# Float64 weights to float32 in three word operations instead of four, the first of them a Prelu on ScalarE

## The chip, the cores and the metric

One core of a Trainium2 chip runs the whole program. The core has a matrix engine (TensorE, PE in the rows; its weight loads are PEld), VectorE (DVE), ScalarE (ACT), GpSimd (POOL) and SyncE (SP), which issues all the DMAs here. The metric is the time of one execution on the device, in microseconds (us).

## The reference

Attention with a decay, then two feed-forward blocks that run over all tokens:

```python
scores = scale * q @ k.T;  decay = cumsum(log(clip(f)))        # 4 batches x 8 heads, 576 x 576, head size 64
x = softmax(causal(scores + decay)) @ v                        # -> 2304 tokens x 512
h = x @ moe_w_in;   x = (h * clip(h + 3, 0, 6) / 6) @ moe_w_out          # 512 -> 2048 -> 512
h = x @ moe2_w_in;  out = softplus(h) @ moe2_w_out                       # 512 -> 2048 -> 512
```

`moe_w_in`, `moe_w_out` and `moe2_w_in` come as float64 after their scaling, and the kernel makes float32 of float64 words itself. All the rest is float32.

## The kernel before

**Stages.** Attention goes through 4 batches of 4 head pairs. The first block runs over token tiles of 512 (the last one 256), with 16 tiles of 128 hidden features each; its first tokens need only batch 0 of the attention, so the matmuls of the block (lines 1299 and 1362) are mixed with the attention's (685, 776, 846) up to some 490 us. The second block, with sums and differences of its tiles prepared in advance (lines 1415 and 1516), fills the span from some 640 us to the end.

**Order.** Every operation is put into a list with its operands, a wish time `at` and one or more ways (an engine with an assumed cost). `Work.order` then sends them one by one to the engine that could start first by these costs, and so writes one fixed order for each engine. On the chip each engine goes through its own list strictly in order, and a semaphore holds it where an operand is not ready. Nothing else sets the times, so an instruction that waits holds up all that stands behind it on its engine.

**Weights.** There are 64 tiles of 128 x 512 float64 words to convert, two 32-bit words each. A tile is loaded by one 512 KB DMA into a staging buffer, `st0` or `st1` for 62 tiles and two places of `HY` for 2; eight of the tiles, of the second block, are converted late, from 570 us on. `raw_weights` converts it in four operations, whose names in the code are:

- `conv0` (line 1016 or 1017): the upper word, read as a float32, times 2^-112, which brings its exponent field to float32's. The planner may choose DVE or ACT; in the order before, 63 of 64 are on ACT.
- `conv1` (line 1019, DVE): the lower word shifted right by 29.
- `conv2` (line 1020, DVE): the upper word shifted left by 3, or'ed with that.
- `conv3` (line 1023, DVE): the sign bit of the upper word, or'ed in.

For the first block `weights` then rounds the tile to the matmul's type on ACT (line 1035) and subtracts that from the tile on POOL (line 1036); only then can the next load into the same staging buffer land. `early2` converts 24 tiles of the second block during the first and stores them to DRAM.

**Around it.** DVE also holds the running minimum of the scores (line 701), the low halves of the transposed probabilities (816), of Q and K (632) and of the hidden activations (1322), the product behind the activation (1341), and copies that the planner may give to ACT or DVE: the rounded hidden tile (1319 on ACT, 1320 on DVE) and copies of the halves of Q and K (643 on ACT, 645 on DVE).

Of the kernel before, what the change touches and what calls it, by code (L numbers as in the profile page):

```python
# [10 lines left out]
U32 = mybir.dt.uint32  # L11
ACTF = mybir.ActivationFunctionType
ALU = mybir.AluOpType
# [36 lines left out]
    pc=794.25,  # L50
# [21 lines left out]
    cvw=29.86,  # L72
# [33 lines left out]
class Work:  # L106
# [11 lines left out]
    def op(self, ways, fn=None, r=(), w=(), after=(), at=0.0, banks=(), hold=(), free=(), nbytes=0, name="", seq=None, from_=0.0, rows=1.0):  # L118


        o = Op()
        o.ways = [ways] if isinstance(ways, tuple) else list(ways)
        o.at, o.banks, o.hold, o.free, o.nbytes, o.name = at, list(banks), hold, free, nbytes, name
        o.deps, o.succ, o.est, o.eng = {}, [], 1000.0 * from_, None
        o.early, o.rows = self.mark, rows
        for b in o.banks:
            b.users += 1
        r, w = list(r) + o.banks, list(w)
        for t in r:
            if t in self.writer:  # L130
                o.deps[self.writer[t]] = 1
        for t in w:
            for d in [self.writer.get(t)] + self.readers.get(t, []):
                if d is not None:
                    o.deps.setdefault(d, 1)
        for t in after:
            for d in [self.writer.get(t)] + self.readers.get(t, []):
                if d is not None:
                    o.deps.setdefault(d, 0)
        if seq:  # L140
            if seq in self.writer:
                o.deps.setdefault(self.writer[seq], 0)
            self.writer[seq] = o
        for t in r:
            self.readers.setdefault(t, []).append(o)
        for t in w:
            self.writer[t] = o
            self.readers[t] = []
        self.ops.append(o)
        return o  # L150
# [123 lines left out]
def attention_two_moe_kernel(  # L274
# [18 lines left out]
    nc = tc.nc  # L293
# [14 lines left out]
    scale = 1.0 / float(D) ** 0.5  # L308
    K = PLAN
# [20 lines left out]
    op = wk.op  # L330
# [6 lines left out]
    def act(n, psum, extra=0):  # L337
        return 0.833 * n + (50 if psum else 93) + 93 * extra

    def dve(n, fast=False, extra=0):  # L340
        return (0.52 if fast else 1.04) * n + 67 + 61 * extra
# [10 lines left out]
    def dma(fn, nbytes, n=1, **kw):  # L352
        return op(("sp", 520.0 * n, fn), nbytes=nbytes, **kw)
# [9 lines left out]
    def moe_at(t, ft):  # L363

        t = min(t, LAST_B - 1)
        return BLK[t] + (BLK[t + 1] - BLK[t]) * (ft / NF) ** (K["cA"] if t == 0 else 1.0)
# [107 lines left out]
    def open_late_pt():  # L474
# [20 lines left out]
        out=bar[:, Z:], in_=bar[:, Z:], compare_op=ALU.is_ge,  # L495
# [472 lines left out]
    def w_source(m, o, ft):  # L968
        w = ((moe_w_in, moe_w_out), (moe2_w_in, moe2_w_out))[m][o]
        e = 2 if wide else 1  # L970
        if o:
            return w[ft * P:(ft + 1) * P, :]
        return w[:, ft * P * e:(ft + 1) * P * e].rearrange("(c p) f -> p c f", p=P)
# [3 lines left out]
    def staging(i):  # L977


        if i < 2:  # L980
            return st[i]
        t = BIG["HY"][:, (i - 2) * 2 * NC * P:(i - 1) * 2 * NC * P] if i < 4 else GT if i == 4 else BIG["rBL"]
        return t.bitcast(U32).rearrange("p (n e) -> p n e", e=2)

    def words(i):

        return staging(i).bitcast(F32).rearrange("p n e -> p (n e)").rearrange("p (e n) -> p e n", e=2)

    def raw_weights(i, m, o, ft, at, dense=False):

        def load():
            dst = staging(i).rearrange("p n e -> p (n e)")
            if not wide:
                dst = dst.bitcast(F32)[:, 0:NC * P]
            if o == 0:
                dst = dst.rearrange("p (c f) -> p c f", c=NC)  # L1000
            nc.sync.dma_start(out=dst, in_=w_source(m, o, ft))

        dma(load, 8 * P * NC * P, w=[("stage", i), ("up", i)] + [("o", i, 0), ("o", i, 1)] * (i < 2), r=["m2"] * (i in (2, 3)), at=at - K["ldw"], name="loadw", from_=K["wfrom"])

        def up():
            return staging(i)[:, :, 1]

        def upf():
            return up().bitcast(F32)

        def low():
            return staging(i)[:, :, 0]

        n = NC * P
        if wide:
            op([("dve", dve(n, True), lambda: nc.vector.tensor_scalar(upf(), upf(), 2.0 ** -112, None, op0=ALU.mult), K["pc"]),
                ("act", act(n, False), lambda: nc.scalar.activation(out=upf(), in_=upf(), func=ACTF.Copy, scale=2.0 ** -112))],
               w=[("up", i)], at=at - K["cvw"], name="conv0")
            op(("dve", dve(n, True), lambda: nc.vector.tensor_scalar(low(), low(), 29, None, op0=ALU.logical_shift_right)), w=[("stage", i)], at=at - K["cvw"], name="conv1")
            op(("dve", dve(n), lambda: nc.vector.scalar_tensor_tensor(  # L1020
                out=low(), in0=up(), scalar=3, in1=low(), op0=ALU.logical_shift_left, op1=ALU.bitwise_or,
            )), r=[("up", i)], w=[("stage", i)], at=at - K["cvw"], name="conv2")
            op(("dve", dve(n), lambda: nc.vector.scalar_tensor_tensor(  # L1023
                out=words(i)[:, 0].bitcast(U32) if dense else low(), in0=up(), scalar=0x80000000, in1=low(), op0=ALU.bitwise_and, op1=ALU.bitwise_or,
            )), r=[("up", i)], w=[("stage", i)] + [("up", i)] * dense, at=at - K["cvw"], name="conv3")

    def weights(o, ft, at):

        i = nw[0] % 2
        nw[0] += 1  # L1030
        raw_weights(i, 0, o, ft, at)
        n = NC * P
        new = ["latew"] if ft >= FW else []
        w = st[i].bitcast(F32)[:, :, 0] if wide else words(i)[:, 0]
        op(("act", act(n, False), lambda: nc.scalar.activation(out=WT[o, ft][0], in_=w, func=ACTF.Copy)), r=[("stage", i)] + new, w=[("W", o, ft, 0)], at=at, name="wh")  # L1035
        op(("pool", pool(n), lambda: nc.gpsimd.tensor_tensor(WT[o, ft][1], w, WT[o, ft][0].bitcast(F32), op=ALU.subtract)),  # L1036
           r=[("stage", i), ("W", o, ft, 0)] + new, w=[("W", o, ft, 1)], at=at, name="wl")
# [30 lines left out]
    def early2(o, ft, at):  # L1068

        i = nw[0] % 2  # L1070
        nw[0] += 1
        raw_weights(i, 1, o, ft, at, True)
        dma(lambda: nc.sync.dma_start(out=wf_dram[o, ft], in_=words(i)[:, 0]), 4 * P * NC * P, r=[("stage", i), ("up", i)], w=[("wf", o, ft)], at=at - K["cvw"], name="storewf")

    def weights2(o, p, at, parts, i0, pace=()):
# [6 lines left out]
        for z in range(2):  # L1082
            i, ft = i0 + z, 2 * p + z
            if not own and (o, ft) in late2:
                raw_weights(i, 1, o, ft, at, True)
                continue

            def load(i=i, ft=ft):
                dst = raw(i) if own else words(i)[:, 0]
                if wide:  # L1090
                    nc.sync.dma_start(out=dst, in_=wf_dram[o, ft])
                else:
                    nc.sync.dma_start(out=dst.rearrange("p (c f) -> p c f", c=NC) if o == 0 else dst, in_=w_source(1, o, ft))

            dma(load, 4 * P * NC * P, w=[("stage", i), ("up", i)] + [("o", i, 0), ("o", i, 1)] * (i < 2), r=["m2"] * (i in (2, 3) or own) + [("wf", o, ft)],
                at=at - 15, name="loadwf")
# [473 lines left out]
    for n in range(len(units) + 1):  # L1570
        if n < len(units):
            t, ft = units[n]
            if (t, ft) == (NB - 2, 0):
# [3 lines left out]
                at = moe_at(t, 0) - K["xl"]  # L1577
# [6 lines left out]
            if ft == NF - 1 and t + 1 < NB - 1:  # L1584

                at = moe_at(t + 1, 0) - K["xl"]
# [85 lines left out]
```

## Time and profile before

| | |
|---|---|
| median of 3 runs | 1022.02 us (1018.5 to 1025.15) |
| the profiled execution's own time | 1020.33 us |
| its span, first to last instruction | 1018.3 us |
| busy: PE, DVE, ACT, POOL | 978.4, 838.2, 599.8, 256.4 us |
| mean granted TensorE clock | 0.993 |

Busy time is the time in which an engine has at least one instruction in work. The ends of matmuls are modelled, so a PE that is busy all the time need not be at its best pace. "The chain" is the chain of work that ended last, followed back from the last instruction through what released each step. A line in a row is that of the kernel before.

### The profile page before, as it was taken

What the parts mean: (1) busy time and instruction counts of PE and PEld (TensorE: products, weight loads), DVE (VectorE), ACT (ScalarE), POOL (GpSimd) and SP (SyncE); (2) the same over time, 40 slices, a digit from 0 to 9 for tenths busy, and PEclk for the clock granted to TensorE, in tenths of its full rate; (3) what the DMA queues carried; (4) which work ended last, traced back from release to release, by engine and by line L of the source; (5) the groups of instructions that cost most, each with busy time, mean ns of one, the idle gap of its engine ahead of it and who ended that gap; (6) DMA issues with size and microseconds to landing.
All of it is one profiled execution on the core that took longest, in us unless ns stands there. A gap on an engine that the chain in (4) does not pass through costs nothing.

```text
span 1018.3 us, 17717 instructions
## 1 busy us (share of the span) xinstructions
PE 978.4 (96%) x6116; PEld 850.4 (84%) x6116; DVE 838.2 (82%) x1662; ACT 599.8 (59%) x1309; POOL 256.4 (25%) x245
## 2 busy tenths in 40 slices
PE   8999999889999999999999999999999999999997
PEld 6566677668788888888888778899999999999997
DVE  8789979998999868998676878787787758888885
ACT  6899766877667557675443545665555544443442
POOL 2221241220000010000345744210010308454442
PEclk9999999999999999999999999999999999999999
DMA  6666553445545526443565660554324994444342
GB/s 138 168 143 157 136 145 94 122 134 153 145 141 144 135 66 177 118 138 104 180 209 178 225 212 21 163 169 141 140 105 164 340 359 134 126 146 145 112 125 77
DMA packets 192066, 153.47 MB, mean 151 GB/s; under 512 B 108220, under 2 KB 163932, under 8 KB 191080
## 3 DMA queue, kind: packets, MB, share of 16 engines
q1 hardware_dynamic: 191976, 152.34, 50.2%
q8 instruction: 48, 0.79, 0.3%
q14 instruction: 42, 0.34, 0.1%
HBM read 99.68 MB, written 52.47 MB: 149 GB/s over the span
## 4 chain that ended last, share of the span: by engine, by line
PE 67%; DVE 19%; issue 5%; ACT 3%; DMA 3%; POOL 2%; SPq 1%; DVEq 0%; POOLq 0%; ACTq 0%
PE bank L1516 16%; PE bank L1415 15%; PE bank L1299 13%; PE bank L1362 13%; PE bank L685 4%; PE bank L846 3%; PE bank L776 3%; DVE MX L1322 2%; DVE st L1020 2%; DVE GT L1341 1%; DVE st L1023 1%; DVE p L701 1%; DMA st<-in_moe_w_in_dram 1%; DVE KB L632 1%; DVE QA L632 1%
## 5 line engine op out<-in xcount | busy, mean ns | idle before, releaser
L1299 PE MATMUL bank<-MX,W 128*128 128x512 f32 x768 | 225.4, 406 | 4.1 <-DVE GT L1341 2.9
L1362 PE MATMUL bank<-MX,W 128*128 128x512 f32 (+1 forms) x688 | 188.4, 382 | 3.5 <-DVE MX L1322 3.5
L1299 PEld LDWEIGHTS bank<-MX,W 128*128 128x128 f32 x768 | 133.7, 191 | 26.6 <-DVE GT L1341 3.9
L1362 PEld LDWEIGHTS bank<-MX,W 128*128 128x128 f32 x688 | 121.6, 189 | 25.5 <-DVE MX L1322 4.1
L1516 PE MATMUL bank<-rW,rW 128*128 128x256 f32 x1134 | 138.6, 283 | 1.3 <-POOL rW L1139 0.9
L1516 PEld LDWEIGHTS bank<-rW,rW 128*128 128x128 f32 x1134 | 136.9, 191 | 2.1 <-POOL rW L1139 1.1
L1415 PE MATMUL bank<-XO,rW 128*128 128x288 f32 x672 | 92.7, 298 | 2.2 <-DVE HY L1433 1.6
L1415 PEld LDWEIGHTS bank<-XO,rW 128*128 128x128 f32 x672 | 90.3, 188 | 4.0 <-DVE HY L1433 2.3
L710 ACT ACTIVATE p<-p,stats 64x64 f32<-64x64 f32 (+4 forms) x130 | 72.2, 556 | 27.8 <-DVE stats L701 26.9
L1495 ACT ACTIVATE rW<-st 128x512 fp32r<-128x512 f32 (+1 forms) x72 | 36.9, 518 | 76.9 <-PE bank L1516 46.5
L1036 POOL TENSOR_TENSOR W<-st,W 128x512 fp32r<-128x512 f32 x24 | 34.9, 1456 | 159.8 <-ACT W L1035 133.8
L1339 ACT ACTIVATE GT<-bank,three 128x512 f32<-128x512 f32 x80 | 51.3, 643 | 39.6 <-DVE MX L1322 18.1
L1415 PE MATMUL bank<-MX,rW 128*128 128x288 f32 x480 | 70.2, 297 | 1.0 <-DVE HY L1433 1.0
L1415 PEld LDWEIGHTS bank<-MX,rW 128*128 128x128 f32 x480 | 65.7, 188 | 1.8 <-DVE HY L1433 1.4
L776 PE MATMUL bank<-ident,p 128*128 128x128 f32 x390 | 58.6, 275 | 8.3 <-DVE xs L861 4.4
L776 PEld LDWEIGHTS bank<-ident,p 128*128 128x128 f32 x390 | 46.2, 140 | 23.9 <-DVE xs L861 4.4
L581 POOL TENSOR_TENSOR V<-vr,V 128x640 fp32r<-128x640 f32 x10 | 17.2, 1718 | 189.3 <-ACT V L577 189.3
L811 ACT ACTIVATE pth<-bank 128x320 fp32r<-128x320 f32 (+2 forms) x100 | 42.3, 433 | 37.4 <-PE bank L776 26.3
L1322 DVE TENSOR_TENSOR MX<-GT,MX 128x512 fp32r<-128x512 f32 (+1 forms) x69 | 51.9, 757 | 13.0 <-ACT MX L1319 12.3
L1499 POOL TENSOR_TENSOR rW<-st,rW 128x256 fp32r<-128x256 f32 (+1 forms) x35 | 41.1, 1178 | 80.8 <-ACT rW L1495 66.5
L1341 DVE SCALAR_TENSOR_TENSOR GT<-GT,bank 128x512 f32<-128x512 f32 x80 | 49.8, 628 | 13.1 <-ACT GT L1339 12.5
L701 DVE CUSTOM_DVE_ANT_0 p<-bank,bar 64x64 f32<-64x64 f32 (+4 forms) x130 | 51.9, 421 | 6.4 <-PE bank L685 5.8
(220 smaller groups left out, 2102.8 us busy)
## 6 DMA issues: line engine op xcount, KB each, us to landing
st<-g_dram SPq DMA_DIRECT2D x36, 512.0 KB
st<-in_moe_w_out_dram SPq DMA_DIRECT2D x32, 512.0 KB
st<-in_moe_w_in_dram SPq DMA_DIRECT2D x30, 512.0 KB
wo_dram<-XO SPq DMA_DIRECT2D x49, 256.0 KB
g_dram<-HY SPq DMA_DIRECT2D x16, 576.0 KB
g_dram<-rBW SPq DMA_DIRECT2D x16, 576.0 KB
rW<-wo_dram SPq DMA_DIRECT2D x5, 1792.0 KB
wf_dram<-st SPq DMA_DIRECT2D x24, 256.0 KB
```

The costliest lines, as they stand in the source:

```text
L701: nc.vector.tensor_tensor_reduce(out=T["P"][par][ti][:r, a:c], in0=bank[bk.i][:r, o:o + c - a], in1=bar[:r, b0:b0 + c - a], op0=ALU.add, o ...
L710: nc.scalar.activation(out=pt, in_=pt, func=ACTF.Exp, scale=-1.0, bias=sv[:r, 0, ti:ti + 1], accum_out=sv[:r, 1, ti:ti + 1],)
L776: nc.tensor.transpose(acc[:, p0:p0 + P], T["P"][par][ti][:, k0:k0 + P], ident)
L811: nc.scalar.activation(out=place("PTH", j, ks, a, c), in_=src(), func=ACTF.Copy)
L1299: nc.tensor.matmul(bank[bk.i][:, 0:n], w[:, c], x[:, c, 0:n], start=(c == 0 and p == 0), stop=(c == NC - 1 and p == 2))
L1322: op(("dve", dve(n), lambda: nc.vector.tensor_tensor(t(glt), g, t(ght).bitcast(F32), op=ALU.subtract)), r=[("g", i), ("gh", i3)], w=[("gl" ...
L1339: op(("act", act(n, True, 1), lambda: nc.scalar.activation(out=g, in_=bank[bk.i][:, 0:n], func=ACTF.Relu, bias=three)), r=["three"], banks ...
L1341: op(("dve", dve(n), lambda: nc.vector.scalar_tensor_tensor(out=g, in0=g, scalar=6.0, in1=bank[bk.i][:, 0:n], op0=ALU.min, op1=ALU.mult)), ...
L1362: nc.tensor.matmul(bank[b][:, o:o + n], w[:, c * P:(c + 1) * P], x, start=(ft == 0 and p == 0 and o == 0), stop=(ft == NF - 1 and p == 2), ...
L1415: nc.tensor.matmul(bank[bks[b].i][:, 0:HA], wa[u][:, c], xa[v][:, c], start=(nm in ("P1", "P2", "P5") and c == 0 and y == 0), stop=(c == 1 ...
L1499: e.tensor_tensor(dst(1), src(), dst(0).bitcast(F32), op=ALU.subtract)
L1516: nc.tensor.matmul(bank[bks[b].i][:, o * 256:(o + 1) * 256], ga[u], wa[v], start=(p == 0 and o == 0 and y == 0), stop=(p == NPR - 1 and y ...
```

## The change

The upper word's sign no longer has its own operation. ACT applies Prelu in place of a plain copy: a positive word is multiplied by 2^-112 as before, a negative one by 2^-112 and then by -2^32. That makes it positive and adds 32 to its float32 exponent field, which sets bit 28 of the word. The shift left by 3, which `conv2` does anyway, moves bit 28 to bit 31, the sign. `conv3` goes away, `conv2` writes the end result, and the DVE way of `conv0` goes away as well.

```diff
         if wide:
-            op([("dve", dve(n, True), lambda: nc.vector.tensor_scalar(upf(), upf(), 2.0 ** -112, None, op0=ALU.mult), K["pc"]),
-                ("act", act(n, False), lambda: nc.scalar.activation(out=upf(), in_=upf(), func=ACTF.Copy, scale=2.0 ** -112))],
+            op(("act", act(n, False), lambda: nc.scalar.activation(out=upf(), in_=upf(), func=ACTF.Prelu, scale=2.0 ** -112, alpha=-(2.0 ** 32))),
                w=[("up", i)], at=at - K["cvw"], name="conv0")
             op(("dve", dve(n, True), lambda: nc.vector.tensor_scalar(low(), low(), 29, None, op0=ALU.logical_shift_right)), w=[("stage", i)], at=at - K["cvw"], name="conv1")
             op(("dve", dve(n), lambda: nc.vector.scalar_tensor_tensor(
-                out=low(), in0=up(), scalar=3, in1=low(), op0=ALU.logical_shift_left, op1=ALU.bitwise_or,
-            )), r=[("up", i)], w=[("stage", i)], at=at - K["cvw"], name="conv2")
-            op(("dve", dve(n), lambda: nc.vector.scalar_tensor_tensor(
-                out=words(i)[:, 0].bitcast(U32) if dense else low(), in0=up(), scalar=0x80000000, in1=low(), op0=ALU.bitwise_and, op1=ALU.bitwise_or,
-            )), r=[("up", i)], w=[("stage", i)] + [("up", i)] * dense, at=at - K["cvw"], name="conv3")
+                out=words(i)[:, 0].bitcast(U32) if dense else low(), in0=up(), scalar=3, in1=low(), op0=ALU.logical_shift_left, op1=ALU.bitwise_or,
+            )), r=[("up", i)], w=[("stage", i)] + [("up", i)] * dense, at=at - K["cvw"], name="conv2")
```

The planner works with the shorter list, so the orders of all engines change in detail. Over the program DVE loses the 64 operations of line 1023 and the one of line 1016. The planner gives it 8 more copies of the hidden tile (39 in place of 31) and 4 more copies of Q and K halves (39 in place of 35), and ACT loses these. Lines after 1023 have numbers lower by 3 in the kernel after.

The first place is DVE's list where the 31st and 32nd weight tiles are converted. In the kernel before (it runs there at 223 to 229 us) it reads, with `st_170` and `st_171` the two staging buffers, `GT` the hidden tile and `MX` its two halves:

```order
L1020 SCALAR_TENSOR_TENSOR st_170<-st_170 128x512
L1341 SCALAR_TENSOR_TENSOR GT<-GT,bank_71 128x512
L1023 SCALAR_TENSOR_TENSOR st_170<-st_170 128x512
L1019 TENSOR_SCALAR st_171<-st_171 128x512
L701 ISA p_152,stats_148<-bank_72,bar 64x64
L701 ISA stats_148 64x1
L1020 SCALAR_TENSOR_TENSOR st_171<-st_171 128x512
L1322 TENSOR_TENSOR MX<-GT,MX 128x512
L1023 SCALAR_TENSOR_TENSOR st_171<-st_171 128x512
```

In the changed kernel the 32nd tile (its line 1319 is the 1322 of before, its 1317 the 1320):

```order
L1019 TENSOR_SCALAR st_171<-st_171 128x512
L701 ISA p_153,stats_148<-bank_76,bar 128x192
L701 ISA stats_148 128x1
L701 ISA p_154,stats_148<-bank_71,bar 128x320
L1020 SCALAR_TENSOR_TENSOR st_171<-st_171 128x512
L701 ISA p_155,stats_148<-bank_72,bar 128x448
L1317 CAST MX<-GT 128x512
L816 TENSOR_TENSOR ptl_1439<-bank_75,pth_1435 128x320
L1319 TENSOR_TENSOR MX<-GT,MX 128x512
```

Line 1023 is gone, other instructions stand between the two conversions, and the copy of the hidden tile has come over from ACT; its low half stands behind `conv2` as before.

The second place is ACT's list where the first softplus of the second block stands, before:

```order
L1430 ACTIVATE rBW<-bank_71 128x288
L1430 ACTIVATE HY<-bank_69 128x288
L1460 ACT_TABLE_LOAD
L1460 ACTIVATE HY<-HY 128x2x288
L1136 ACTIVATE rW_5871<-st_170 128x1024
```

and in the changed kernel:

```order
L1427 ACTIVATE rBW<-bank_71 128x288
L1427 ACTIVATE HY<-bank_69 128x288
L1457 ACT_TABLE_LOAD
L1457 ACTIVATE HY<-HY 128x2x288
L1133 ACTIVATE rW_5809<-st_170 128x1024
```

This load and the one at the very start (line 491) are the only two table loads of either list; none stands beside a Prelu.

## Rows read from the trace of the kernel before

**Rows 1.** The page: busy time of each engine, share of the span, instructions.
```profile
PE 978.4 (96%) x6116; PEld 850.4 (84%) x6116; DVE 838.2 (82%) x1662; ACT 599.8 (59%) x1309; POOL 256.4 (25%) x245
```

**Rows 2.** The chain over the whole span: shares by engine (page) and by line.
```profile
PE 67%; DVE 19%; issue 5%; ACT 3%; DMA 3%; POOL 2%; SPq 1%; DVEq 0%; POOLq 0%; ACTq 0%
...
by line: PE bank L1516 15.7%; PE bank L1415 14.8%; PE bank L1299 12.9%; PE bank L1362 12.7%; issue 5.2%; PE bank L685 3.7%; PE bank L846 3.5%; PE bank L776 3.4%; DVE MX L1322 1.7%; DVE st L1020 1.7%; DVE GT L1341 1.2%; DVE st L1023 1.2%; DV
```

**Rows 3.** Busy time (and instructions) of each engine in three stretches.
```profile
core 0: us, PE busy (x) PEld busy (x) DVE busy (x) ACT busy (x) POOL busy (x), PEclk, DMA share, GB/s
...
100.00:225.00 125.00, 114.36 (x592) 87.81 (x591) 111.19 (x234) 90.96 (x201) 34.20 (x23) 1.00 0.47 127
225.00:475.00 250.00, 243.81 (x1309) 201.85 (x1308) 220.88 (x523) 168.85 (x388) 16.02 (x10) 0.99 0.48 133
475.00:650.00 175.00, 167.94 (x937) 143.84 (x936) 127.67 (x194) 79.78 (x173) 74.29 (x79) 0.99 0.54 172
```

**Rows 4.** The same stretches for line 1023 alone: DVE busy (instructions), clock, DMA.
```profile
100.00:225.00 125.00, 17.64 (x21) 1.00 0.47 127
225.00:475.00 250.00, 17.98 (x25) 0.99 0.48 133
475.00:650.00 175.00, 7.40 (x9) 0.99 0.54 172
```

**Rows 5.** The chain by line, from 100 to 225 us and from 225 to 350.
```profile
by line: issue 11.8%; DVE st L1020 10.0%; PE bank L1299 9.5%; DVE st L1023 7.5%; PE bank L1362 6.1%; PE bank L846 5.9%; DVE MX L1322 5.9%; DVE p L701 3.6%; PE bank L776 3.2%; PE bank L685 3.1%; DVE KB L632 3.0%; DVE st L1019 3.0%; DVE QA L6
...
by line: PE bank L1299 28.2%; PE bank L1362 24.5%; PE bank L685 9.5%; PE bank L776 8.2%; PE bank L846 5.0%; issue 4.7%; DVE st L1020 2.6%; DVE KB L632 2.4%; DVE MX L1322 2.3%; DVE xs L861 2.2%; DVE QA L632 1.8%; DVE st L1023 1.2%; DVE qkt L
```

**Rows 6.** Groups: count, busy us, mean ns of one, idle before and what ended it.
```profile
L1023 DVE SCALAR_TENSOR_TENSOR st<-st 128x512 uint32<-128x512 uint32 x62 | 47.9, 773 | 0.7
L1020 DVE SCALAR_TENSOR_TENSOR st<-st 128x512 uint32<-128x512 uint32 x62 | 46.5, 751 | 4.9 <-ACT st L1017 3.4
L1339 ACT ACTIVATE GT<-bank,three 128x512 f32<-128x512 f32 x64 | 43.8, 686 | 28.1 <-PE bank L1299 11.5 <-DVE MX L1322 10.1 <-DVE SB L1322 5.5
L1017 ACT ACTIVATE st<-st 128x512 f32<-128x512 f32 x61 | 41.1, 675 | 8.4 <-DMA st<-in_moe_w_in_dram 7.4 <-DMA st<-in_moe_w_out_dram 0.8
L1320 DVE CAST MX<-GT 128x512 fp32r<-128x512 f32 x28 | 12.9, 462 | 15.3 <-PE bank L1362 14.8
L645 DVE CAST QB<-QA 64x576 fp32r<-64x576 f32 x18 | 12.9, 718 | 0.1
```

**Rows 7.** Pieces of the chain from 140 to 230 us: start, us, what.
```profile
147.72 1.68 DVE st L1023
...
159.81 0.69 DVE st L1023
...
176.32 1.73 DVE st L1023
...
215.60 1.18 DVE st L1023
```

**Rows 8.** Timeline at 226 us: start, us, engine, line, operation, [idle before <- releaser].
```profile
225.70 0.69 DVE L1020 SCALAR_TENSOR_TENSOR st<-st 128x512 uint32<-128x512 uint32 x1
...
226.04 1.50 POOL L1036 TENSOR_TENSOR W<-st,W 128x512 fp32r<-128x512 f32 x1 [4.73 <-ACT W L1035]
...
226.31 1.78 DVE L1322 TENSOR_TENSOR MX<-GT,MX 128x512 fp32r<-128x512 f32 x1
...
228.14 1.22 PE L1362 MATMUL bank<-MX,W 128*128 128x512 f32 x2 [2.27 <-DVE MX L1322]
```

**Rows 9.** Two short stretches, columns as in rows 3.
```profile
228.20:235.20 7.00, 7.00 (x22) 5.59 (x23) 4.65 (x15) 3.13 (x9) 1.30 (x1) 0.62 0.31 91
535.00:545.00 10.00, 8.21 (x39) 6.91 (x38) 5.17 (x7) 1.32 (x4) 5.70 (x7) 0.83 0.57 191
```

**Rows 10.** Line 1460, softplus: ns min/median/max of one, first and last start.
```profile
L1460 ACT ACTIVATE HY<-HY x32: 668/685/688, 650.8 to 827.2; 128x576 f32<-128x576 f32 x32
...
L1460 ACT ACT_TABLE_LOAD  x1: 1283/1283/1283, 649.5 to 649.5; - x1
```

## The prediction, made before the changed kernel ran

> **What bounds the kernel now.** I first read the busy times. PE has 96% and DVE 82% of the span [rows 1], which makes DVE look harmless; but the share is a mean over stages. So the second view is the chain of work that ended last. PE holds 67% of it and DVE 19%, and line 1023, the operation that goes, has 1.2% [rows 2]: 12.2 us of 1018.3. The third view says where. From 100 to 225 us DVE is busy 111.2 of 125 us, PE 114.4 and ACT 91.0; from 225 to 475 us DVE has 220.9 of 250, but PE 243.8; from 475 to 650 us DVE has 127.7 of 175 [rows 3]. The chain by stretch agrees: from 100 to 225 us it goes again and again through DVE, with 7.5% of it on line 1023, while from 225 to 350 us lines 1299 and 1362 on PE hold more than half and line 1023 has 1.2% [rows 5]. In us that is 9.4 and 1.5; the other 1.3 of the 12.2 lie elsewhere. So the reader is to see one stage in which DVE's list sets the pace, followed by longer ones in which it mostly runs beside PE.
>
> **The change, part by part.**
>
> *Line 1023 goes.* Its 62 operations on `st` take 47.9 us of DVE [rows 6], of which 17.6 lie in 100 to 225 us, 18.0 in 225 to 475 and 7.4 in 475 to 650 (this stretch with the two on `HY`) [rows 4]. A saving on the path can't be read from these sums: in the second stretch 18.0 us of work appear with about 1.5 us in the chain, as PE and ACT cover the rest. I take the chain's share, 12.2 us.
>
> *Part of that passes to another instruction.* Undisturbed, the operation takes 0.69 us; on the chain it took 1.68, 1.73 and 1.18 us at three places [rows 7], 2.5 us more than three times 0.69. The timeline at 226 us shows what such a stretch is: POOL's subtraction (line 1036) starts at 226.04 and takes 1.50 us, DVE's line 1322 starts at 226.31, and takes 1.78 us, past POOL's end [rows 8]. Another DVE operation with two tensor inputs is thus held in the same way. POOL's 32 subtractions stay, and whichever such DVE operation meets one pays. So I take these 2.5 us off: 12.2 - 2.5 = 9.7 us. The other end is that nothing is passed on, 12.2 us.
>
> The Trainium skill's page SBUF — State Buffer (Who interferes with whom) says the same as a rule: a DVE instruction with two SBUF inputs and a GpSimd instruction that reads SBUF exclude each other, and the later one is fully blocked. It speaks against counting a collision as saved; by it the sum ends at 9.7 us, and with the bare chain it would be 12.2. The 1.78 us beside POOL's 1.50 agree with it.
>
> *Prelu for Copy.* The trace has no Prelu. The nearest rows on ACT are Copy, 0.675 us for 512 elements (line 1017), the Relu with a bias from PSUM, 0.686 (line 1339) [rows 6], and softplus, 0.685 for 576 elements, so an estimated 0.61 for 512 [rows 10]. I take Copy's 0.675, since operand and place are the same; the ends are 64 x (-0.065) = -4.2 and 64 x 0.011 = 0.7 us on an ACT that has 34 us free in the first stretch and 81 in the second [rows 3]: nothing on the path. The one `conv0` that DVE had goes to ACT.
>
> *Copies that come over to DVE.* Eight of the hidden tile at 0.462 us and four of Q and K halves at 0.718 [rows 6] are 3.7 + 2.9 = 6.6 us. They come from the planner finding room on DVE, and ACT loses as many. I cost them at nothing: the 18.0 us that line 1023 leaves in 225 to 475 us cover them. Were that cover gone, they would cost up to 6.6 us. At the other end, a shorter ACT list could bring up to as much; I take no gain from it, as ACT has only 3% of the chain.
>
> *The new orders.* All lists are rewritten, and the relative pace of attention and the first block stays close to what it was. Waits go and come with that, PE's among them. The nearest price is the stall at 228 us: PE stood 2.27 us for line 1322 [rows 8], and then ran 7.0 us at a mean granted clock of 0.62 [rows 9], between its levels of 1.2 and 2.4 GHz, which costs 7.0 x 0.38 = 2.7 us more. One such episode is 5.0 us. It may vanish (a gain of 5.0) or get a twin (a loss of 5.0); I count zero, and keep both ends.
>
> Sum: the profiled execution took 1020.33 us (span 1018.3 and 2.0 around it), so 1020.33 - 9.7 = 1010.6, **1011 us**. The median of the runs shown is 1.7 us higher, and the runs spread over 6.7 us, so this offset is within what runs differ by; against the median of 1022.0 it is 1.1% less. What can be told from no change is about 1%, or 1011.8 and 1032.2 us as the bounds.
>
> **The rivals.**
>
> *PE is given back all that it waits (chance 0.21).* If DVE's list was what PE waited for in all the mixed stages, PE's idle time goes: 125 - 114.4 = 10.6 and 250 - 243.8 = 6.2 us [rows 3], and with it the clock loss of 2.7 us: 19.5 us, 1001 us. With the 7.1 us of 475 to 650 us it is 994. For it speaks that DVE is loaded to 89% in the first stretch and loses 16% of that load. Against it speaks "issue" with 11.8% of the chain there, and that a part of PE's waits is for ACT and for weights.
>
> *Something else takes the place (0.25).* The conversion of a tile still runs from the load through ACT, DVE, ACT and POOL, and removing 18.0 us of DVE in 225 to 475 us takes little off the chain. If the same holds in 100 to 225 us, because line 1020, with 10.0% of the chain [rows 5], or PE ends there instead, perhaps 2 to 3 us remain: 1018 us, 1015 to 1026 with the copies or one stall on top.
>
> *Slower: DVE stands for ScalarE in front of work that PE needs (0.11).* `conv2` (line 1020) waits for ACT's product. With a shorter list in front DVE gets there earlier; before, it waited for line 1017 for 3.4 us in all [rows 6]. Behind it stand, in the place shown, the copy and the low half of a hidden tile that PE's matmuls need. If ACT is late there, DVE stands, PE stands behind it, and its clock falls as after 226 us. Each such episode costs 5.0 us. Before, there are two low stretches, at 228 and at 535 us (clock 0.83 there) [rows 9]. The gain is eaten by two more, and slower by 1% needs (1032.2 - 1010.6) / 5.0, so five: 1010.6 + 25 = 1036 us. Against it speaks that 63 of 64 products were on ACT already and that ACT has a quarter of the first stretch free.
>
> *ScalarE must change its tables (0.01).* If Prelu were not in the set that Exp and Copy use, loads at 1.283 us [rows 10] would stand around the 64 conversions, two each: 164 us more, 1184 us. The built order has the same two loads as before, so this is all but excluded. The Trainium skill's page ScalarE: Activation LUTs (Table sets: the hidden batching unit) says that functions come in named sets and a change of set costs a load, and does not name Prelu among the functions it lists.
>
> **How the numbers follow.** My forecast has 0.42, between 1004 and 1016 us; with its middle at 1011, 0.25 of it lie below 1011.8 and 0.17 above. Faster by over 1%: 0.21 + 0.25 = 0.46. Within 1%: 0.17 + 0.25 = 0.42. Slower: 0.11 + 0.01 = 0.12. The range reaches down to 996 us, into the first rival by most of its width, and up to 1026 us, the upper end of the second; outside are the slower cases with 0.12 and some 0.06 of the first rival. Cases of both signs do not share the chance evenly, but the forecast's own range stands above.
>
> **What the profile after would show.** Line 1023 is gone and DVE's busy time is lower by 47.9 - 6.6, some 41 us. Line 1017 stays near 0.675 us. From 100 to 225 us of work the same matmuls take some 9 us less, and line 1020 and 1322 show as many stretched instances as before or more. The share of DVE in the chain falls from 19% by about one point. If the second rival is right, DVE's idle time in that stage grows by what was taken out, with PE or ACT as releaser. If the slower one is, line 1020's waits for ACT grow well over 3.4 us and the clock shows more than two low stretches. I am wrong by the largest amount if the new orders move PE's waits more than the operation itself was worth, since their sum is counted as zero here.

## The result and the profile after

The changed kernel takes 1012.65 us (median of 7 runs, 1006.57 to 1014.28). The ratio to the kernel before, which ran beside it, is 0.9907 with an interval of 0.9883 to 0.9931: 0.9% or some 9.5 us faster, just inside the 1% that the prediction took as the bound of what can be told apart. One of the seven runs of the kernel before, of 2934.95 us, is left out of the ratio. Timed once more the changed kernel took 1009.64 us, ratio 0.9890 (0.9866 to 0.9914). The forecast was 1011 us and a saving of 9.7 us. The sum came out, but, as the experiments show, two of its terms did not.

The profiled execution took 1014.28 us, with a span of 1012.4 and a mean granted clock of 0.991. Its page, in the columns of [rows 1] and [rows 2]:

```profile
PE 979.8 (97%) x6116; PEld 852.4 (84%) x6116; DVE 802.0 (79%) x1615; ACT 591.0 (58%) x1295; POOL 248.8 (25%) x242
...
PE 68%; DVE 18%; DMA 4%; issue 4%; ACT 3%; POOL 1%; SPq 1%; DVEq 0%; POOLq 0%; ACTq 0%
```

DVE lost 36.2 us of busy time, and its share of the chain went from 19% to 18%. The windows of [rows 3] in the kernel after, behind them the seven microseconds of [rows 9], and last a stretch near the start:

```profile
core 0: us, PE busy (x) PEld busy (x) DVE busy (x) ACT busy (x) POOL busy (x), PEclk, DMA share, GB/s
...
100.00:225.00 125.00, 118.58 (x601) 91.38 (x601) 104.90 (x232) 94.33 (x210) 33.77 (x24) 0.99 0.51 136
225.00:475.00 250.00, 247.93 (x1361) 206.79 (x1360) 207.46 (x510) 164.62 (x383) 12.77 (x8) 1.00 0.46 130
475.00:650.00 175.00, 168.00 (x935) 143.49 (x935) 124.90 (x192) 80.44 (x172) 70.31 (x78) 0.99 0.54 174
...
228.20:235.20 7.00, 6.99 (x37) 5.59 (x36) 5.85 (x15) 3.97 (x11) 0.00 (x0) 1.00 0.19 45
...
11.30:21.50 10.20, 10.20 (x29) 6.94 (x28) 5.38 (x20) 6.34 (x21) 0.00 (x0) 0.50 0.82 190
```

PE's idle time fell by 4.2 us in the first stretch (118.58 against 114.36) and by 4.1 in the second (247.93 against 243.81), and not at all in the third. The low clock at 228 us (0.62 in [rows 9]) is gone. A smaller episode of the same kind stands at 170 us in the kernel after, where PE waits 1.97 us for line 1338 and then runs 3.4 us at 0.50 (a row of the timeline, then one of the windows):

```profile
170.46 0.96 PE L1296 MATMUL bank<-MX,W 128*128 128x512 f32 x3 [1.97 <-DVE GT L1338]
...
171.70:175.10 3.40, 3.40 (x14) 2.76 (x13) 2.92 (x10) 1.01 (x4) 0.00 (x0) 0.50 0.04 11
```

Near the start, too, PE ran from 11.3 to 21.5 us at a granted clock of 0.50, its level of 1.2 GHz, on work that both kernels have in the same order. The timeline of PE there, in the kernel after (start, us, engine, line, operation, idle time before it):

```profile
9.43 3.58 PE L685 MATMUL bank<-KF,QF 97*128 97x192 f32 x10 [2.76 <-DVE KF L606]
...
13.45 6.03 PE L685 MATMUL bank<-KF,QF 97*128 97x192 f32 x12
```

and in the kernel before:

```profile
9.43 2.79 PE L685 MATMUL bank<-KF,QF 97*128 97x192 f32 x10 [2.56 <-DVE KF L606]
...
12.96 3.31 PE L685 MATMUL bank<-KF,QF 97*128 97x192 f32 x12
```

The same twelve matmuls take 6.03 us in place of 3.31. This execution is 4.3 us behind, by the starts of the same matmuls, before PE has met the change. Its net saving can be read from one operation that both kernels have: the last group of softmax operations on DVE (line 701) and the first matmuls of the second block. The rows give ns of one (min/median/max) and the first and last start. After:

```profile
L701 DVE CUSTOM_DVE_ANT_0 p<-bank,bar x130: 152/453/626, 10.8 to 464.6; 64x64 f32<-64x64 f32 x26, 128x192 f32<-128x192 f32 x26, 128x320 f32<-128x320 f32 x26, 128x448 f32<-128x448 f32 x26
...
L1412 PE MATMUL bank<-XO,rW x672: 290/297/406, 636.2 to 777.1; 128*128 128x288 f32 x168
```

Before:

```profile
L701 DVE CUSTOM_DVE_ANT_0 p<-bank,bar x130: 203/453/626, 10.8 to 471.1; 64x64 f32<-64x64 f32 x26, 128x192 f32<-128x192 f32 x26, 128x320 f32<-128x320 f32 x26, 128x448 f32<-128x448 f32 x26
...
L1415 PE MATMUL bank<-XO,rW x672: 290/297/404, 643.0 to 783.0; 128*128 128x288 f32 x168
```

The last line-701 operation starts 6.5 us earlier, the second block 6.8 us earlier. So everything was gained before 471 us (10.8 us, with the 4.3 lost at the start added back) and nearly nothing after it.

The chain by line from 100 to 225 us, for [rows 5]:

```profile
by line: PE bank L1296 15.3%; PE bank L1359 13.4%; issue 13.0%; PE bank L846 7.6%; PE bank L685 6.4%; DMA st<-in_moe_w_in_dram 4.9%; PE bank L776 4.0%; DVE MX L1319 3.8%; DVE st L1019 2.5%; DVE ptl L816 2.4%; DVE st L1020 2.2%; DVE GT L1338
```

Line 1020 fell from 10.0% to 2.2%, and PE's lines lead. The groups, for [rows 6]:

```profile
L1020 DVE SCALAR_TENSOR_TENSOR st<-st 128x512 uint32<-128x512 uint32 x62 | 45.2, 730 | 4.4 <-ACT st L1017 3.2
...
L1319 DVE TENSOR_TENSOR MX<-GT,MX 128x512 fp32r<-128x512 f32 x59 | 48.0, 816 | 3.2 <-ACT MX L1316 2.4
...
L1017 ACT ACTIVATE st<-st 128x512 f32<-128x512 f32 x62 | 41.8, 676 | 7.5 <-DMA st<-in_moe_w_in_dram 4.6 <-DMA st<-in_moe_w_out_dram 2.4
...
L1317 DVE CAST MX<-GT 128x512 fp32r<-128x512 f32 x36 | 16.0, 446 | 23.4 <-PE bank L1359 23.1
```

and the row of the kernel before that answers to line 1319:

```profile
L1322 DVE TENSOR_TENSOR MX<-GT,MX 128x512 fp32r<-128x512 f32 x59 | 45.8, 777 | 3.1 <-ACT MX L1319 2.4
```

Prelu takes 676 ns where Copy took 675. Line 1020 waits no longer for ACT than before (3.2 against 3.4 us).

### The profile page after: what moved, and what is told of

Read it like the earlier page. It is cut to its first block, busy times and chain, and to the rows that moved or that the text cites. A ratio compares the mean times of both kernels' runs of the same rounds, so it can differ in the third digit from the quotient of the medians.

```text
span 1012.4 us, 17646 instructions
## 1 busy us (share of the span) xinstructions
PE 979.8 (97%) x6116; PEld 852.4 (84%) x6116; DVE 802.0 (79%) x1615; ACT 591.0 (58%) x1295; POOL 248.8 (25%) x242
## 4 chain that ended last, share of the span: by engine, by line
PE 68%; DVE 18%; DMA 4%; issue 4%; ACT 3%; POOL 1%; SPq 1%; DVEq 0%; POOLq 0%; ACTq 0%
PE bank L1513 15%; PE bank L1412 14%; PE bank L1296 13%; PE bank L1359 13%; PE bank L685 6%; PE bank L846 4%; PE bank L776 4%; DMA st<-in_moe_w_in_dram 2%; DVE MX L1319 2%; DVE GT L1338 1%; DMA st<-in_moe_w_out_dram 1%; DVE p L701 1%; DVE rW L1136 1%; DVE st L1020 1%; DVE KB L632 1%
## 5 line engine op out<-in xcount | busy, mean ns | idle before, releaser
L1319 DVE TENSOR_TENSOR MX<-GT,MX 128x512 fp32r<-128x512 f32 (+1 forms) x69 | 53.8, 784 | 13.1 <-ACT MX L1316 12.4
L776 PEld LDWEIGHTS bank<-ident,p 128*128 128x128 f32 x390 | 48.1, 144 | 14.7 <-DVE ptl L816 1.6
```

What stands on the lines that cost most here:

```text
L776: nc.tensor.transpose(acc[:, p0:p0 + P], T["P"][par][ti][:, k0:k0 + P], ident)
L1319: op(("dve", dve(n), lambda: nc.vector.tensor_tensor(t(glt), g, t(ght).bitcast(F32), op=ALU.subtract)), r=[("g", i), ("gh", i3)], w=[("gl" ...
```

## Experiments

The theory in front of the runs was that of the prediction: the operation is worth its part of the chain, and a collision with POOL passes on to a neighbour. The rivals were that the gain comes from the new orders rather than from the operation, and that DVE was past what PE can cover, so that a saving or an addition is worth far more, or far less, than the chain's share. All twelve were timed in five rounds. In the table, "us saved" is (1 - ratio) times the median of the kernel before beside it (1020.45, 1021.0 and 1020.19 us in the three sets).

| run | what differs | us | ratio, 95% interval | us saved |
|---|---|---|---|---|
| e0_after_again | the changed kernel | 1009.64 | 0.9890 [0.9866, 0.9914] | 11.2 |
| e1_order_before | the change in the old order | 1007.15 | 0.9863 [0.9838, 0.9888] | 14.0 |
| e2_order_after | new order, old operations | 1051.33 | 1.0292 [1.0265, 1.0319] | -29.8 |
| e3_one_less | e1, one more operation gone | 1003.01 | 0.9822 [0.9798, 0.9847] | 18.2 |
| e4_late8_only | gone for the 8 late tiles | 1018.11 | 0.9977 [0.9958, 0.9996] | 2.3 |
| e5_first56_only | gone for the other 56 | 1007.78 | 0.9879 [0.9852, 0.9906] | 12.4 |
| e6_block1_only | gone for the first block's 32 | 1013.28 | 0.9931 [0.9906, 0.9956] | 7.0 |
| e7_sign_twice | line 1023 twice | 1070.06 | 1.0475 [1.0444, 1.0506] | -48.5 |
| e8_order_before_warm | e1 and 7 more matmuls at the start | 1005.88 | 0.9858 [0.9833, 0.9882] | 14.5 |
| e9_no_read | before, POOL's subtractions don't read | 1012.43 | 0.9933 [0.9908, 0.9958] | 6.8 |
| e10_no_read_no_sign | e1, the same | 1008.45 | 0.9878 [0.9851, 0.9905] | 12.4 |
| e11_after_warm | after and 7 more matmuls at the start | 1011.09 | 0.9902 [0.9877, 0.9928] | 10.0 |

**The operation and the orders apart.** The planner gets the list of before, with line 1023's entry and its cost, but the entry issues nothing; Prelu stands where the product stood and line 1020 writes the end result. The orders of PE, POOL and SP are those of before; ACT has one operation more, DVE 65 fewer.

```diff
-            op([("dve", dve(n, True), lambda: nc.vector.tensor_scalar(upf(), upf(), 2.0 ** -112, ...), K["pc"]),
-                ("act", act(n, False), lambda: nc.scalar.activation(..., func=ACTF.Copy, scale=2.0 ** -112))],
+            op([("dve", dve(n, True), prelu, K["pc"]), ("act", act(n, False), prelu)],
...
-            op(("dve", dve(n), lambda: nc.vector.scalar_tensor_tensor(...)), ..., name="conv3")
+            op(("dve", dve(n), lambda: None), ..., name="conv3")
```

> The changed conversion (Prelu, no sign operation) in the order of the kernel before: the planner still counts the removed operation, and nothing is issued in its place. If the gain is the work that DVE no longer has on the path (my theory), this gains what was forecast, 8 to 12 us: ratio 0.988 to 0.992. If the gain of the changed kernel comes from its new orders (rival), this gains 0 to 3 us: 0.997 to 1.000, and PE's stall at 228 us stays.

It saves 14.0 us: more than the changed kernel did. By the interval that is 11.4 to 16.5 us, so it can't be told from line 1023's 12.2 us of the chain. The windows of e1:

```profile
100.00:225.00 125.00, 119.10 (x611) 92.88 (x610) 100.49 (x228) 94.99 (x216) 35.45 (x25) 0.99 0.49 133
225.00:475.00 250.00, 248.80 (x1362) 207.50 (x1361) 204.63 (x496) 169.60 (x387) 13.12 (x8) 1.00 0.47 134
475.00:650.00 175.00, 169.25 (x970) 146.76 (x969) 130.29 (x196) 87.05 (x185) 78.30 (x83) 1.00 0.55 176
```

PE's idle time falls by 4.7 us in the first stretch and 5.0 in the second; in the third there is 1.3 too, which the kernel after lacks. The share of PE in its chain is 75%, DVE's 14%:

```profile
PE 75%; DVE 14%; issue 3%; ACT 3%; DMA 2%; SPq 1%; POOL 1%; DVEq 0%; ACTq 0%; POOLq 0%
```

The place of [rows 8] in e1 (line 1022 is the 1020 of before; from line 1025 on numbers are as before):

```profile
219.35 0.71 DVE L1022 SCALAR_TENSOR_TENSOR st<-st 128x512 uint32<-128x512 uint32 x1
...
219.96 0.70 DVE L1322 TENSOR_TENSOR MX<-GT,MX 128x512 fp32r<-128x512 f32 x1
...
220.25 1.58 POOL L1036 TENSOR_TENSOR W<-st,W 128x512 fp32r<-128x512 f32 x1 [4.68 <-DMA x_dram<-xs]
...
220.72 1.10 PE L1362 MATMUL bank<-MX,W 128*128 128x512 f32 x2 [0.59 <-DVE MX L1322]
```

Line 1322 now starts ahead of POOL's subtraction and takes 0.70 us in place of 1.78; PE stands 0.59 us for it in place of 2.27. Its clock falls here too, but for a shorter time:

```profile
220.90:224.30 3.40, 3.40 (x10) 2.75 (x10) 2.23 (x8) 1.79 (x7) 2.22 (x2) 0.50 0.39 135
```

That is the episode priced at 5.0 us. At half speed 3.4 us cost 1.7, so an estimated 0.59 + 1.7 = 2.3 us of it are left in e1, and the rest went with the operation itself. The rows show one thing more: line 1322 starts 0.61 us after line 1022, whose own time is given as 0.71. Neighbours on DVE overlap by some 0.1 us, so 65 operations less take less off the busy time than the sum of their durations (here 838.2 - 792.8 = 45.4 us).

The other half is the order of after with the work of before: line 1020's entry issues both old operations.

```diff
+            def two():
+                nc.vector.scalar_tensor_tensor(out=low(), in0=up(), scalar=3, in1=low(), op0=ALU.logical_shift_left, op1=ALU.bitwise_or)
+                nc.vector.scalar_tensor_tensor(out=..., in0=up(), scalar=0x80000000, in1=low(), op0=ALU.bitwise_and, op1=ALU.bitwise_or)
...
+            op(("dve", dve(n), two), ..., name="conv2")
```

> The four operations of before (Copy on ScalarE, sign operation on DVE right behind the or) in the order of the changed kernel. My theory: the order alone is worth nothing, and this is at the time of the kernel before or above it, since its lists were made without the operation: 1.000 to 1.008. The rival (the new order is the gain): 0.990 to 0.995.

1051.33 us, 29.8 slower than before and 41.7 slower than the same order with the short list. Its windows:

```profile
100.00:225.00 125.00, 109.48 (x526) 83.12 (x525) 105.54 (x213) 82.42 (x184) 32.62 (x22) 0.95 0.43 117
225.00:475.00 250.00, 239.84 (x1271) 194.76 (x1271) 216.66 (x508) 160.65 (x366) 15.77 (x10) 0.99 0.47 129
```

PE's idle time rises in both stretches and the clock falls to 0.95 in the first. So the operation is worth 14.0 us in the old order and 41.7 in the new one. Undoing the edit in the new order alone would have shown about four times what the change brought (9.5 and 11.2 us). The gain does not come from the orders.

The changed kernel itself ran in the same set, without an edit:

> The changed kernel beside the three others on the same chip, for their comparison. Both theories: 0.988 to 0.993. In its profiled execution TensorE's clock was at its lower level for 10.2 us near the start, on work that the two kernels share; if that belongs to single executions and not to the order, it is not there in every execution, and the mean clock of the fastest runs is higher.

1009.64 us, 2.5 us behind e1; the two intervals overlap.

**Where the operation counts.** In the order of before, it is left out for some of the tiles only:

```diff
+            gone = m == 1 and (o, ft) in late2          # e4; e5: not that; e6: m == 0
...
+            def last():
+                if not gone:
+                    sign(end())
```

> In the order of the kernel before, the sign operation is gone only for the 8 tiles converted after 570 us; the other 56 keep all four operations. If the 4.8 us that the first kernel gained between 471 and 650 us come from these 8 tiles (my theory now: the weight path of the second block waits for them), this gains 3 to 5 us: ratio 0.995 to 0.997. If the chain's share is right (1.2 us there) and that gain came from being earlier or from the clock, 0 to 1.5 us: 0.9985 to 1.000.

> The opposite half: in the order of before, gone for the 56 tiles up to 500 us, kept for the 8 late ones. My theory: 9 to 11 us, ratio 0.989 to 0.991, all of it there by 300 us. If the late gain is a consequence of the early one, the whole 14 us: 0.986 to 0.987.

> In the order of before, gone only for the 32 tiles of the first block (up to 230 us), whose path goes on through ScalarE and GpSimd to the matmuls. If the gain is in the stretch up to 230 us, where VectorE sets the pace, 6 to 10 us: 0.990 to 0.994. If it is spread over all tiles alike, half of 14: 0.993. If the tiles of the second block that are converted among them count as much (they load the same list), 3 to 6 us: 0.994 to 0.997.

The parts add up: 2.3 + 12.4 = 14.7 against 14.0. The first block's 32 tiles, converted up to 229 us, give 7.0 us; the 24 that follow, by difference, 5.4; the 8 late ones 2.3. The intervals are some 2.5 us to each side, so these are sizes, not exact shares. The late tiles' part shows where it should: in e4 the last line-701 operation starts 1.9 us later than in before (473.0), the second block 2.8 us earlier (640.2). But the chain had put 9.4 in 100 to 225 us and 1.5 in the stretch behind it.

**How near the edge the kernel before stood.** One operation more, and one operation less, both in the order of before. e7 issues line 1023 twice (`sign(low()); sign(end())`). e3 is e1 without the shift of the lower word (line 1019), and with an `and` in place of line 1020's `or`; its weights are other numbers altogether, so only its time is of use:

```diff
-            op(("dve", dve(n, True), lambda: nc.vector.tensor_scalar(low(), low(), 29, ..., op0=ALU.logical_shift_right)), ..., name="conv1")
+            op(("dve", dve(n, True), lambda: None), ..., name="conv1")
...
-                out=low(), ..., op0=ALU.logical_shift_left, op1=ALU.bitwise_or,
+                out=..., ..., op0=ALU.logical_shift_left, op1=ALU.bitwise_and,
```

> In the order of before, the sign operation is issued twice for all 64 tiles (the second does the same again). If each operation of VectorE costs the same in either direction, 14 us slower: 1.014. If it is a bottleneck there, the loss grows beyond the gain, towards the operations' own 50 us: 1.025 to 1.045. If it were mostly hidden and the 14 us came from elsewhere, under 5 us: below 1.005.

> As the first, in the order of the kernel before, with the shift of the lower word (0.43 us of DVE per tile) left out as well, so the weights' values are not the reference's. If DVE's list still sets the pace in the mixed stage, a further 3 to 6 us against the first kernel of this set: ratio 0.983 to 0.988. If the first removal already used up what DVE held on the path, 0 to 2 us: within 0.002 of the first kernel.

The chain of e7 by engine, and its stretch from 100 to 225 us by line (1025 is the doubled operation, 1036 the 1020 of before):

```profile
PE 56%; DVE 30%; issue 6%; ACT 3%; DMA 2%; POOL 2%; SPq 1%; DVEq 0%; POOLq 0%; ACTq 0%
...
by line: DVE st L1025 16.3%; issue 11.0%; DVE st L1036 10.4%; PE bank L1313 8.4%; DVE MX L1336 4.6%; DVE st L1035 3.8%; DVE GT L1355 3.2%; DVE p L701 3.0%; PE bank L846 2.9%; DVE QB L645 2.8%; PE bank L685 2.8%; PE bank L776 2.6%; ACT st L1
```

64 operations more cost 48.5 us, 0.76 us each: as much as they last (769 ns on average in that trace). 64 less bring 14.0 us, 0.22 us each. 64 of line 1019 less, of some 0.42 us each, bring another 4.2 us (some 3.5 to either side, by the two intervals), 0.07 each. The kernel before stood where DVE's list begins to set the end: what is added counts several times as much as what is taken away. That the 48.5 us equal the durations of the operations is no proof that each counts in full. The busy times of e7 show that the 51 us by which its span is longer are of two kinds:

```profile
PE 1001.2 (94%) x6116; PEld 861.1 (81%) x6116; DVE 887.9 (83%) x1726; ACT 601.8 (56%) x1309; POOL 256.7 (24%) x245
```

PE's idle time is 28 us longer than before, and its busy time 23 us, on the same matmuls at a mean granted clock of 0.977 in place of 0.993.

**Whether collisions pass on.** POOL's 32 subtractions (line 1036) become fills with zero, which read nothing, so the low halves of the first block's weights are left out. A fill also takes POOL 0.52 us in place of some 1.4, and the staging buffer is free for the next load earlier.

```diff
-        op(("pool", pool(n), lambda: nc.gpsimd.tensor_tensor(WT[o, ft][1], w, WT[o, ft][0].bitcast(F32), op=ALU.subtract)),
+        op(("pool", pool(n), lambda: nc.gpsimd.memset(WT[o, ft][1].bitcast(F32), 0.0)),
```

> The kernel before, with GpSimd's 32 subtractions replaced by fills with zero, which read nothing (the low halves of the first block's weights are left out, so the output isn't the reference's). It shows what all collisions of VectorE with them cost. My forecast counted on a collision as time on the path: if so, this gains 5 to 10 us, 0.990 to 0.995, and the stretched instances of lines 1020, 1023 and 1322 go. If collisions are as good as free, 0 to 2 us (the weights are ready 0.8 us earlier): 0.998 to 1.000.

> The same with the changed conversion in the order of before. If the operation that went passed its collisions on to others (my forecast), taking them away is worth more here or as much as in the kernel before: 0.978 to 0.982 against before. If its share of the collisions went with it, the two gains overlap, and this lies only 2 to 4 us below the first kernel: 0.982 to 0.985.

The edit does one thing more. A fill waits for no weight, so the first ones run from 6.20 us on, and DVE's line 618, which runs beside some of them, takes 2.28 us; in before it starts at 8.03 and takes 0.45. In e9:

```profile
6.20 1.45 POOL L1036 MEMSET W<- 128x512 f32 x3
...
8.02 2.28 DVE L618 COPY KF<-vr 1x576 f32<-1x576 f32 x1
...
8.07 1.46 POOL L1036 MEMSET W<- 128x512 f32 x3
...
11.25 2.47 PE L685 MATMUL bank<-KF,QF 97*128 97x192 f32 x6 [4.46 <-DVE KF L606]
```

PE's first matmuls of line 685 start 1.8 us later than in before (9.43), in e9 and e10 alike. This loss is no cost of the subtractions, and both results contain it.

With the operation in place, e9 is 6.8 us faster, or an estimated 8.6 with the 1.8 added back. Its groups:

```profile
L1020 DVE SCALAR_TENSOR_TENSOR st<-st 128x512 uint32<-128x512 uint32 x62 | 44.4, 716 | 5.2 <-ACT st L1017 3.7
L1023 DVE SCALAR_TENSOR_TENSOR st<-st 128x512 uint32<-128x512 uint32 x62 | 43.2, 697 | 0.7
```

Line 1023 takes 697 ns in place of 773. Without the operation, taking the reads away gains nothing that can be seen in the time (e10 0.9878 against e1's 0.9863), though PE's idle time from 100 to 225 us is 2.7 us in e10 and 5.9 in e1. The two edits do not add up: 6.8 + 14.0 would be 20.8, and 12.4 is measured; with the 1.8 us, 22.6 against 14.2. Two limits: the runs of e10 had a granted clock of 0.986 to 0.995, those of e1 0.992 to 0.998, and half a per cent of clock is up to 5 us, so a rest of that size may be hidden; and the fill is shorter, frees the buffer earlier and reads nothing, so the gain of e9 is not the collisions alone.

Whether collisions pass on can also be counted in the traces. Lines 1020, 1023 and 1322 of before have 192 operations of 128x512. 26 of them start while POOL is in an operation with two tensor inputs, and take 1.32 us on average; none of the other 166 takes more than 0.70. Of the 26, 10 belong to line 1023 and 16 to the other two. In e1 these other two have 15 such operations, in the kernel after 18. So in the old order no collision passed on, and in the new one two did. That the 15 of e1 cost little because they lie beside work of PE is my reading.

**The low clock at the start.** Of the twelve profiled executions without more matmuls there, eight show a stretch of 3.4 to 10.2 us at 0.50 that begins at 9 to 13 us (after, e3, e4, e5, e6, e7, e9 and e10), four do not (before, e0, e1, e2). Kernels with the same PE list stand on both sides (e1 and e3, after and e0), so it is not the change. Seven more matmuls on the identity stand behind the last one that warms PE up, in both orders:

```diff
+    for y in range(K["nwarm"]):
+        op(("pe", 213.0, lambda y=y: [nc.tensor.matmul(bank[0][:, 0:P], ident, ident) for _ in range(8 if y == K["nwarm"] - 1 else 1)]), ..., name="warm")
```

> The first kernel (changed conversion in the order of before) with 7 more of the matmuls that TensorE does at the start on nothing, in the 2.8 us in which it waits for the first transposed K; all orders stay. In several profiled executions, of different kernels, TensorE's clock went to its lower level for 3 to 10 us from about 10 us on, and cost up to 4 us. If TensorE's standing still before that is the cause, it does not happen here: the median is 1 to 3 us below the first kernel's, 0.983 to 0.985 against before, and the runs lie closer together. If not, the same 0.986, or 0 to 1.5 us more where the matmuls get in the way.

> The changed kernel with the 7 more matmuls at the start, in its own order, to hold against the first kernel of this set with the noise of the start taken out. If the new orders cost something against the old ones, it is slower than that one by 2 to 4 us: 0.986 to 0.988 against before. If the difference so far (2.5 us, with overlapping intervals) was chance, the two agree within 1 us.

Neither profile has the stretch. The median of e8 is 1.3 us below e1's, that of e11 1.45 above e0's: no gain that can be told. The runs of e8 spread over 2.3 us against 5.5 of e1. Two profiles and this spread fit a removed dip, but don't prove it. How long PE stands ahead of it doesn't decide it: 1.34 us in e5, where the clock fell, and 2.37 in e0 and 2.56 in before, where it didn't.

What the pair does show is the price of the new orders: e11 is 5.2 us behind e8 (their runs don't meet: 1008.45 to 1012.91 against 1004.59 to 1006.84), and e0, less clearly, 2.5 behind e1. The groups of e8, where the operations stand in the old order:

```profile
L1022 DVE SCALAR_TENSOR_TENSOR st<-st 128x512 uint32<-128x512 uint32 x62 | 45.6, 736 | 7.4 <-ACT st L1017 5.8
L1322 DVE TENSOR_TENSOR MX<-GT,MX 128x512 fp32r<-128x512 f32 x59 | 43.8, 743 | 7.2 <-ACT MX L1319 6.5
```

Line 1322 takes 743 ns here, 777 in before and 816 in after. The old order leaves the freed time as idle time in front of these two groups (14.6 us, where before had 8.0); in the new one other operations stand there, and line 1319 meets POOL more often (13 of its 128x512 operations start while POOL is in one with two inputs, 9 of line 1322's in e8).

**The fastest version** is e1 with the seven matmuls, 1005.88 us, ratio 0.9858 (0.9833 to 0.9882); e1 alone, 1007.15 us, can't be told from it. Both beat the kernel before, and the runs of e8 lie below all of e11, the changed kernel with the same matmuls.

## Why the prediction was right, step by step

*The bound.* That DVE sets the pace in the first stretch and is covered later was half right. The first block's tiles gave 7.0 us where 9.4 was read, the 24 behind them 5.4 where the second stretch had 1.5 [rows 5]. In that second stretch PE's idle time of 6.2 us fell to 1.2 in e1, although the chain showed little of line 1023 there. 2.27 us of the 6.2 are the wait at 228 us, which in e1 is shorter and falls ahead of 225. That PE otherwise waited there for operations that stood behind line 1023 in DVE's list, of which the chain names only the last, is my reading; no run tests it.

*Line 1023 goes, 12.2 us.* This term held as far as can be told: 14.0 us, between 11.4 and 16.5, in the order that the 12.2 was read from. The 9.7 that the next step left of it lie below.

*Collisions pass on, -2.5 us.* This step failed in the old order. The collisions of the other two lines went from 16 to 15 there, line 1322 fell to 743 ns, and without POOL's reads no more could be seen in the time. It held in part in the new one, with 18 collisions, where line 1319 rose by 39 ns, 2.3 us over 59, while line 1020 fell by 1.3. The rule of the Trainium skill's page SBUF — State Buffer (Who interferes with whom), that a DVE instruction with two SBUF inputs and a GpSimd instruction that reads SBUF shut each other out, still fits the rows (1.78 us against 0.70). Wrong was my use of it: that the collisions of the operation that goes are taken over by the ones that stay.

*Prelu, the table loads and the copies, 0.* Prelu was as taken (676 ns). The 12 copies cost nothing that shows before 471 us: PE gained there nearly as much as in e1 (8.3 against 9.7 us of idle time).

*The new orders, 0, between -5.0 and 5.0.* Mis-sized: they cost 2.5 to 5.2 us, from half of the -5.0 to just past it. Of the prediction's price, the episode at 228 us, an estimated 2.3 us are left in e1 and nothing in the kernel after, so more than half of what vanished belongs to the first term. The twin came too: the 1.97 us of waiting and 3.4 us at 0.50 at 170 us, an estimated 3.7 us together; e0 waits there as long and its clock stays up. Of the rest of the loss most lies behind the last line-701 operation. From there to the second block e1 gains another 4.8 us on before (starts at 459.3 and 626.4 us), e8 2.8 (458.0 and 627.1), after only 0.3. The same lists give 2.2 us in e0 (459.2 and 628.9) and lose 0.2 in e11 (461.0 and 633.1), so it differs by execution. PE's waits are the longer ones there, 3.1 us of 580 to 620 us in after against 0.7 in e8:

```profile
580.00:620.00 40.00, 36.87 (x204) 30.76 (x203) 30.84 (x43) 18.71 (x37) 17.37 (x18) 1.00 0.43 134
...
580.00:620.00 40.00, 39.31 (x226) 33.83 (x225) 31.39 (x44) 19.34 (x36) 17.65 (x16) 1.00 0.35 109
```

What makes them is open: a load of a late tile stands in the chain of after (6.86 us at 597.67) and of e11, but also in that of e8 (5.60 us), and no run moved it.

Together: 14.0 less 2.5 to 5.2 is 8.8 to 11.5 us, around the 9.5 and 11.2 measured. Two errors, 4.3 us too little for the operation with its collisions and 2.5 to 5.2 too much for the orders, have cancelled; that the sum came out so close is luck.

*The tests.* Line 1023 gone, line 1017 and DVE's share of the chain came as said. DVE's busy time fell by 36.2, not 41: operations overlap. The 9 us less between 100 and 225 us came as 4.2 to 4.7 of PE's idle time; by the starts of line 1020's operation of [rows 8] the work up to there is 6.4 us shorter in e1 (219.35 against 225.70). The stretched instances were more for line 1319 and fewer for 1020.

*The rivals.* PE was not given back all its waits: 6.4 and 2.1 us of 10.6 and 6.2 remain in after. Something else taking the place would have left 2 to 3 us; 14.0 in the unchanged order excludes it. DVE standing for ACT did not come: 3.2 us at line 1020, and 5.8 in e8, the fastest kernel that computes the whole. The table loads did not come.

## What to carry to other kernels

Here an operation's share of the chain told what its removal brings (12.2 us, measured 14.0), in the order it was read from and no other; change the work in the old order first (an entry that issues nothing), and then let the planner rewrite. Doubling the operation is a cheap second reading: here it cost 48.5 us where removing it brought 14.0, so the engine stood at the edge. The removal was worth a third of what it took off DVE's busy time (45.4 us), and the next one, e3, less (4.2 of 24.0). An order written for the short list was bad with the long one (41.7 us), so undoing an edit under the new order overstates it.

## What had not been expected of the hardware

PE's clock stood at 0.50 for up to 10.2 us near the start, and in another execution of the same list not at all; it cost 4.3 us in the profile of after, nearly half of the effect in question. PE had stood 2.76 us shortly ahead of it there, and 2.56 in before, where the clock stayed up, so the standing alone does not tell when it happens. And the same operation, with the same neighbours, took 1.78 us or 0.70, by whether it started 0.27 us after POOL's subtraction or 0.29 us before it. The count over the trace of before says the same: of the operations of lines 1020, 1023 and 1322 only those that start inside a two-input operation of POOL are stretched, and the 10 beside which POOL starts second take no longer than the rest.
